# One shared score unit for the last two head groups of the last segment: 80 units in place of 81

## The chip, the cores and the metric

The kernel runs on one core of a Trainium2 chip. The metric is the device time of one execution in microseconds. A core has five engines that work side by side, each through its own instructions in order: TensorE (PE, matrix products), VectorE (DVE), ScalarE (ACT), GpSimd (POOL) and SyncE (SP, which here only issues DMA transfers). Their results meet in the on-chip memories SBUF and PSUM; an instruction that needs another engine's or a transfer's result waits on a semaphore.

## What is computed

One block of a model on 2048 tokens of width 640, in bf16. The tokens are normalised; `s` is an attention with 32 heads of width 20, in 4 segments of 512 tokens; `g` is a gated product of width 1536; the result is `x + s * g`.

```python
xn = layernorm(x)
for n in range(4):                       # segments of 512 tokens, 32 heads
    logits = q[n] @ k[n].T * scale + mask          # causal
    a_dot = softmax(logits) @ v[n]
    a_mem = (phi(q[n]) @ M) / (phi(q[n]) @ z + 1e-6)
    o[n] = g * a_mem + (1 - g) * a_dot             # g = sigmoid(beta), per head
    M, z = M + phi(k[n]).T @ v[n], z + sum(phi(k[n]))
s = o @ wo
h = sigmoid(xn @ w_gate) * (xn @ w_up)
out = x + s * silu(h @ w_down)
```

## The kernel before, in words

**Score units.** The 32 heads are 8 groups of 4. In a segment, a group has four key blocks of 128 keys; key block `kb` is seen by the queries from `128*kb` on, so the blocks have 512, 384, 256 and 128 query columns. Blocks are packed into units of up to 512 columns: block 0 alone, blocks 1 and 3 together, and block 2, which has 256 columns, together with block 2 of the neighbouring group. `pair_units` does this for two groups (5 units), `single_units` for one group (3 units, the last with 256 columns). For each unit, `scores` (L548) writes the products of four heads into the one PSUM tile `Sps`, `exps` has ScalarE take the exponential into a tile `pt` (L556, one instruction for the whole unit) and GpSimd mask each block's diagonal (L558).

**Using the units.** For all groups but the last two of the last segment, `attend_T` multiplies a group's `pt` tiles with the values once all its units are there, in the transposed form `ApsT` (L572); VectorE turns the result in blocks of 32 (L593), GpSimd and VectorE divide it, and VectorE turns it back into `obT` (L591). From there it goes to DRAM by `dot_spill` (L473) and back by `out_load` (L480, L483), as the left operand `oT` of the output product.

The last two groups of the last segment, 6 and 7, go another way, through `attend` (L612): unit by unit, into a PSUM tile `Aps` with queries on the partitions. When the group's fourth block is in, `finalize` (four VectorE instructions, L631 to L638) divides and adds the result to `odot`, which holds the memory part of the same rows. For group 7 `finalize` comes in two halves: the first two query blocks after the third key block, the others after the fourth.

**The tail.** `tail_spill` (L510) writes columns 384 to 511 of `odot` to DRAM, `tail_T` (L514) loads them transposed into `oTm`, `tail_sum` (L518, VectorE) adds what `oT` has for these rows. Columns 512 to 639 are transposed on TensorE by `tail_T4` (L523) and copied by ScalarE (L524). Then `tail_piece` makes the output product of the last segment in eight pieces of 128 tokens by 320 columns (L532, five matmuls each, the fourth with `oTm`), and multiplies it with `aa` on VectorE (L534). `tail_add` (L540) adds `x` and the rows are stored.

**The order of the work.** One slot belongs to each unit. A slot begins with the unit's scores and exponentials; the rest of it is filled with dense work from a queue: gate, up and down products of the four segments (5, 5 and 12 matmuls each; a down product is evacuated by a ScalarE instruction, L454, and then a VectorE one, L455). All else (projections, output products, spills, loads, the steps above) is an event with a time in slots; at its time in a slot, as a share of the slot's free work, it is put into the order. The planner has a cost for each piece of work; the sum over the number of slots is the `rate` that a slot is due.

```python
    SLOTS, SEG = len(units), 20
    LAST = (NSEG - 1) * SEG
    OLD = LAST + 15
    ...
    for slot in range(OLD, SLOTS - 1):
        at(slot + 1 + TIMES["attend"], 500, old_attend, slot)
    ...
    rate = (sum(k * c for _, k, c, _ in dense) + sum(e[2] for e in events) + AV_NS * len(visits)) / SLOTS
    ...
    fill(1e12)
    finish(held[1][3])
    tail_T4(0, 2)
    old_attend(SLOTS - 1)
    tail_piece(0, 0)
```

So the slots 75 to 80 hold the units of groups 6 and 7; `old_attend` of a unit comes 0.36 of a slot into the slot that follows its own, and the last unit's after all slots. The event times are written by hand in `TIMES`: of those in the last segment, `dot5` (`dot_spill` of groups 4 and 5) stands at slot 78.0, `load5` (their `out_load`) at 78.1, `add5` at 79.05. Segments 0 to 2 have 20 slots each before and after the change. The down products of the last 128 tokens are held back for the tail (`held`).

## Time and profile before

| what | value |
|---|---|
| median of 3 runs | 320.56 us (319.78 to 628.22) |
| profiled execution: span from the first to the last instruction | 317.6 us |
| what lies around the span, to the median | 2.96 us |
| TensorE busy | 309.7 us, 98% |
| VectorE, ScalarE, GpSimd busy | 229.5, 227.2, 135.5 us |
| granted TensorE clock | 0.999 |
| exponentials (L556) | 81, 150.3 us in all |
| slots 75 to 80 begin (first score matmul) | 285.23, 289.23, 291.81, 294.99, 298.08, 301.37 us |
| first matmul of the first output piece | 306.39 us |

The span is one execution taken by the hardware profiler; the runs are timed without it. An engine's busy time is no cost by itself: what counts is whether the engine that sets the end had to wait. In the lines of the trace, the first number is the start in us from the start of the span, the second the duration, and the bracket, where there is one, says how long the engine was idle before and what it waited for.

### The profile page before, as it was taken

The page shows a single profiled execution, that of the slowest core. Times are in us where ns is not written, and L with a number is a line of the kernel's source. Part 1 is how long each engine was busy: PE and PEld are TensorE (multiplying, and loading weights), DVE is VectorE, ACT ScalarE, POOL GpSimd, SP SyncE. Part 2 cuts the span into 40 slices and gives each one's busy share as a digit, 9 for nine tenths or more (in the row PEclk, how much of TensorE's full clock was granted, in tenths as well). Part 3 has the DMA queues.
Part 4 walks back from the last instruction along what each step waited for, and adds up shares of the span by engine and source line. Part 5 has one row for each costly group of instructions (what it writes and reads, how often), then busy time and mean ns, then how long its engine had stood idle before and what let it go on. Part 6 is the DMA issues. An engine that isn't in the chain of part 4 may idle for free.

```text
span 317.6 us, 10049 instructions
## 1 busy us (share of the span) xinstructions
PE 309.7 (98%) x4215; PEld 167.1 (53%) x4244; DVE 229.5 (72%) x505; ACT 227.2 (72%) x229; POOL 135.5 (43%) x230
## 2 busy tenths in 40 slices
PE   8999999999999999999999999999999999999995
PEld 3544445665555445654665455545466645445673
DVE  6474356755869888997779999977787686734565
ACT  3723477788898877778898868678897766777631
POOL 1870036535263445334453354444533353535322
PEclk9999999999999999999999999999999999999999
DMA  7984886420752462505954443238533000350302
GB/s 252 364 328 142 289 221 191 105 46 2 215 158 62 130 130 85 126 23 173 240 168 122 114 110 109 82 121 210 168 82 120 19 23 23 114 137 4 99 20 83
DMA packets 56085, 41.36 MB, mean 130 GB/s; under 512 B 26952, under 2 KB 54664, under 8 KB 56040
## 3 DMA queue, kind: packets, MB, share of 16 engines
q1 hardware_dynamic: 53496, 35.97, 39.7%
q10 hardware_dynamic: 2544, 4.75, 4.0%
q8 instruction: 33, 0.54, 0.7%
q14 instruction: 12, 0.10, 0.1%
HBM read 19.90 MB, written 14.78 MB: 109 GB/s over the span
## 4 chain that ended last, share of the span: by engine, by line
PE 96%; issue 1%; ACT 1%; DVE 1%; ACTq 0%
PE yp L130 11%; PE up L130 11%; PE gp L130 10%; PE psq L130 10%; PE Sps L548 9%; PE gp L134 6%; PE up L134 6%; PE yp L134 6%; PE psv L130 6%; PE ApsT L572 5%; PE psq L134 4%; PE sp L130 3%; PE sp L134 3%; PE sp L532 2%; PE psv L134 1%; PE wps L644 1%
## 5 line engine op out<-in xcount | busy, mean ns | idle before, releaser
L556 ACT ACTIVATE pt<-Sps 128x2048 bf16<-128x2048 f32 (+1 forms) x81 | 150.3, 1856 | 40.8 <-PE Sps L548 35.9
L558 POOL TENSOR_SCALAR_AFFINE_SELECT pt<-pt 128x512 bf16<-128x512 bf16 x128 | 83.2, 665 | 157.6 <-ACT pt L556 157.5
L438 DVE SCALAR_TENSOR_TENSOR hT<-tg,up 128x512 bf16<-128x512 bf16 x48 | 32.4, 675 | 23.2 <-PE up L130 8.7
L130 PE MATMUL up<-xnT,Wu 128*128 128x512 bf16 x147 | 40.3, 380 | 1.2 <-issue 1.0
L130 PE MATMUL yp<-Wd,hT 128*128 128x320 bf16 x257 | 40.1, 300 | 0.0
L427 ACT ACTIVATE tg<-gp 128x512 bf16<-128x512 f32 x48 | 28.6, 596 | 14.4 <-PE gp L130 11.0
L130 PE MATMUL gp<-xnT,Wg 128*128 128x512 bf16 x144 | 38.1, 379 | 0.3 <-issue 0.2
L548 PE MATMUL Sps<-QT,KT 23*128 23x128 bf16 (+3 forms) x512 | 32.6, 301 | 0.2
L591 DVE STREAM_TRANSPOSE obT<-ob 128x512 bf16<-128x512 bf16 x30 | 21.1, 705 | 13.4 <-POOL ob L587 13.3
L130 PEld LDWEIGHTS <-hT 128*128 128x128 bf16 x257 | 23.5, 98 | 11.6 <-issue 3.0
L455 DVE SCALAR_TENSOR_TENSOR aa<-t,yp 128x320 bf16<-128x320 bf16 x32 | 15.3, 480 | 13.8 <-ACT t L454 13.7
L134 PE MATMUL gp<-xnT,Wg 128*32 128x512 bf16 x360 | 24.1, 380 | 0.0
L548 PEld LDWEIGHTS <-KT 23*128 23x128 bf16 x512 | 10.0, 92 | 24.5 <-issue 24.1
L130 PEld LDWEIGHTS <-Wu 128*128 128x128 bf16 x160 | 14.3, 98 | 16.2 <-issue 3.2
L593 DVE STREAM_TRANSPOSE tb<-ApsT 128x512 f32<-128x512 f32 x30 | 21.2, 708 | 2.2 <-PE ApsT L572 2.1
L572 PE MATMUL ApsT<-pt,V 128*32 128x512 bf16 (+2 forms) x480 | 22.7, 299 | 0.0
L130 PEld LDWEIGHTS <-Wg 128*128 128x128 bf16 x150 | 14.1, 98 | 16.0 <-issue 1.9
L134 PE MATMUL up<-xnT,Wu 128*32 128x512 bf16 x320 | 21.7, 380 | 0.0
L454 ACT ACTIVATE t<-yp 128x320 bf16<-128x320 f32 x32 | 13.9, 435 | 10.2 <-PE yp L130 8.5
L130 PE MATMUL psv<-Wv,xnT 128*128 128x320 bf16 x130 | 20.6, 299 | 0.2
L587 POOL TENSOR_TENSOR ob<-tb,rb 128x320 bf16<-128x320 f32 x27 | 19.8, 733 | 2.3
L134 PE MATMUL yp<-Wd,hT 128*32 128x320 bf16 x508 | 20.0, 300 | 0.0
(122 smaller groups left out, 448.7 us busy)
## 6 DMA issues: line engine op xcount, KB each, us to landing
KT<-Kd SPq DMA_DIRECT2D x32, 80.0 KB
QT<-Qd SPq DMA_DIRECT2D x32, 80.0 KB
out_dram<-xt SPq DMA_DIRECT2D x14, 160.0 KB
Wg<-in_B_w_gate_dram ACTq DMA_DIRECT2D x1, 1920.0 KB
Wu<-in_B_w_up_dram ACTq DMA_DIRECT2D x1, 1920.0 KB
xt<-in_A_x_dram SPq DMA_DIRECT2D x3, 640.0 KB
Wd<-in_B_w_down_dram SPq DMA_DIRECT2D x1, 1920.0 KB
Xd<-xn SPq DMA_DIRECT2D x12, 160.0 KB
```

The lines of the kernel that those rows point to most:

```text
L130: nc.tensor.matmul(out_, lhsT=lhsT, rhs=rhs, start=start, stop=stop, skip_group_check=True)
L134: nc.tensor.matmul(out_[cols], lhsT=lhsT[:, cols], rhs=rhs, start=start, stop=stop, tile_position=(0, 32 * r), skip_group_check=True)
L427: nc.scalar.activation(tg[:], gp[:], ACT.Tanh, scale=0.5)
L438: nc.vector.scalar_tensor_tensor(out=h[:], in0=seg[n]["tg"][:], scalar=1.0, in1=up[:], op0=ALU.add, op1=ALU.mult)
L455: nc.vector.scalar_tensor_tensor(out=s["aa"][j][:, hs], in0=t2[:], scalar=1.0, in1=yp[:], op0=ALU.add, op1=ALU.mult)
L548: nc.tensor.matmul(Sps[:, r, c0:c0 + ncol], lhsT=KT[32 * r:32 * r + DH + 3, g, kb * P:(kb + 1) * P], rhs=QT[32 * r:32 * r + DH + 3, g, q0: ...
L556: nc.scalar.activation(pt[:, :, 0:ntot], Sps[:, :, 0:ntot], ACT.Exp, scale=SCALE)
L558: nc.gpsimd.affine_select(out=pt[:, :, c0:c0 + P], in_=pt[:, :, c0:c0 + P], compare_op=ALU.is_ge, fill=0.0, base=0, pattern=[[0, 4], [1, P ...
L572: nc.tensor.matmul(ps[32 * r:32 * r + 32, q0:L], lhsT=Vflat[n % 2][:, off:off + 32], rhs=t[:, r, c0:c0 + ncol], start=(i == 0), stop=(i == ...
L587: nc.gpsimd.tensor_tensor(ob[:, :, 0:DH], tb[:, :, 0:DH], rb[:].unsqueeze(2).to_broadcast([P, L // 32, DH]), op=ALU.mult)
L591: nc.vector.transpose(s["obT", g // 4][:, g % 4, :], ob[:].rearrange("p b e -> p (b e)"))
L593: s["turn", g] = (lambda: nc.vector.transpose(tb[:].rearrange("p b e -> p (b e)"), ps[:]), quotients, turn_back)
```

## The change

The last pair of groups in the last segment is packed like all the others: one unit holds the third key blocks (`kb` 2) of groups 6 and 7, where each had a unit of 256 columns. The list has 80 units. Group 7's blocks now come to `attend` in the order 2, 0, 1, 3 in place of 0, 1, 3, 2, and its last unit holds blocks 1 and 3. Two of the three tail events have other distances from the end.

```diff
-def single_units(g):
-    return [[(g, 0, 0, 512, 0)],
-            [(g, 1, 0, 384, 128), (g, 3, 384, 128, 384)],
-            [(g, 2, 0, 256, 256)]]
-
 def segment_units(n):
     units = []
     for g in range(0, NG, 2):
-        last = n == NSEG - 1 and g == NG - 2
-        units += single_units(g) + single_units(g + 1) if last else pair_units(g)
+        units += pair_units(g)
     return units
...
-    at(SLOTS - 2.001, 0, tail_spill)
-    at(SLOTS - 1.001, 0, tail_T)
+    at(SLOTS - 1.45, 0, tail_spill)
+    at(SLOTS - 0.9, 0, tail_T)
     at(SLOTS - 0.001, 0, tail_sum)
```

The lines after the slots stay as they are: `tail_T4(0, 2)` is in the order ahead of the last `old_attend`, which now holds both halves of group 7's `finalize`.

## The prediction

> **What bounds the kernel now.** I read first the page's busy times and the chain that ended last. They say the same: TensorE is busy nearly all the time, and the chain is made of its matmuls.

> ```profile
> PE 309.7 (98%) x4215; PEld 167.1 (53%) x4244; DVE 229.5 (72%) x505; ACT 227.2 (72%) x229; POOL 135.5 (43%) x230
> ...
> PE 96%; issue 1%; ACT 1%; DVE 1%; ACTq 0%
> ```

> So time is won only where a TensorE cost goes away, and lost wherever TensorE is made to wait. The list of waits shows how little it waits now: 1.2 us at the start, then nothing above 1.0 us in total. The granted clock is 0.999, so no clock effect stands behind this.

> Next I read the last 30 us in order of time, for each engine alone, because the change acts there. SyncE's queue first, then VectorE, ScalarE and TensorE (start, duration, instruction, idle time before it).

> ```profile
> 294.84 1.42 SPq L473 DMA_DIRECT2D OTd<-obT  x4
> ...
> 297.64 0.39 SPq L480 DMA_DIRECT2D oT<-OTd  x1
> 298.09 0.48 SPq L483 DMA_DIRECT2D oT<-OTd  x1
> 299.52 0.40 SPq L510 DMA_DIRECT2D Od<-odot  x1
> 301.69 1.16 SPq L514 DMA_TRANSPOSE oTm<-Od  x1
> ```

> ```profile
> 294.10 0.71 DVE L591 STREAM_TRANSPOSE obT<-ob 128x512 bf16<-128x512 bf16 x1 [1.25 <-POOL ob L587]
> ...
> 297.74 0.49 DVE L455 SCALAR_TENSOR_TENSOR aa<-t,yp 128x320 bf16<-128x320 bf16 x1 [2.50 <-ACT t L454]
> 298.14 0.25 DVE L631 RECIPROCAL rd<-Aps 128x16 f32<-128x16 f32 x1
> ...
> 299.17 0.33 DVE L638 TENSOR_TENSOR odot<-odot,od 128x320 bf16<-128x320 bf16 x1
> ...
> 306.12 0.42 DVE L518 TENSOR_TENSOR oTm<-oTm,oT 96x512 bf16<-96x512 bf16 x1 [0.51 <-DMA oTm<-Od]
> ```

> ```profile
> 295.50 1.88 ACT L556 ACTIVATE pt<-Sps 128x2048 bf16<-128x2048 f32 x1 [0.78 <-PE Sps L548]
> 297.27 0.43 ACT L454 ACTIVATE t<-yp 128x320 bf16<-128x320 f32 x1
> ```

> ```profile
> 296.28 0.35 PE L612 MATMUL Aps<-V,pt 128*128 128x21 bf16 x8
> ...
> 306.39 0.57 PE L532 MATMUL sp<-Wo,oT 128*128 128x320 bf16 x3
> ```

> The reader is to see one chain here. The attend that completes group 6 starts on TensorE at 296.28. `finalize` (L631 to L638) ends at 299.50, `tail_spill` (L510) is issued at 299.52, `tail_T` (L514) at 301.69, when the spill has landed, and `tail_sum` (L518) starts at 306.12, when the transposed block has landed. TensorE needs that block in the fourth matmul of the first output piece, at 306.80. This chain is 10.5 us long and ends 0.26 us before it is needed. It is invisible in the list of TensorE's waits, and it has no slack.

> **The change part by part.**

> *The merged unit.* The time from the last matmul before a unit to the first after it, less that last matmul's own streaming, is 0.318 us for either unit of 256 columns, 0.438 us for a unit of two 256-column blocks elsewhere in the trace, and 0.424 us for one of 512. Two units at 0.318 become one at 0.438: minus 0.20 us of TensorE. Nothing else leaves TensorE: the matmuls of `attend`, the gate, up and down products are all still there. On ScalarE two exponentials of 1.02 us become one of 1.88; ScalarE is 72% busy, so that is worth nothing by itself.

> *The planner's rate.* The planned work is 240.05 us over 81 slots, 2.964 us each; afterwards 239.55 over 80 (one `old_attend` of 0.5 less), 2.994 each. Dense work runs 31 ns per slot further ahead, 2.3 us by slot 75. I worked the planner's sums through for both lists; for the kernel before, the order that comes out is the trace's. Afterwards the order of segments 0 to 2 is the same but for a few matmuls that stand on the other side of an event. Cost: the next score unit waits for the exponential, which starts about 0.53 us after the scores and takes 1.88, so a slot under 2.46 us stalls. The shortest slots before are 2.46 to 2.62 us; afterwards slot 19 has 2.01 us planned, 2.45 with its scores. That is a stall of a tenth or two; I take 0.2 us in all, between 0 and 0.5.

> *The tail, one slot shorter.* Counted from the attend that completes group 6 (call it a; 296.28 before), TensorE's work up to the fourth matmul of the first piece was: 8 attend matmuls 0.20, 11 down matmuls 1.49 (0.136 each), scores 0.44, 7 down 0.95, 16 attend 0.41, 11 down 1.49, scores 0.32, 7 down 0.95, 16 attend 0.41, 23 down 3.12, two transposes 0.11, 8 attend 0.20, three pieces 0.41: 10.5 us, as the trace has it. Afterwards it is 0.20 + 1.49 + 0.44 + 0.95 + 24 attend 0.61 + 3.12 + 0.11 + 16 attend 0.41 + 0.41 = 7.7 us.

> *The chain in the new order.* `finalize` is no longer held: in the new order no down product is evacuated right ahead of it, so it starts at a + 0.36 and ends at a + 1.7 (1.36 long). But `tail_spill` is queued on SyncE behind `dot_spill(4,6)` and `out_load`, and these wait for group 5's last transpose (L591). In the new order that transpose stands behind the evacuation of a down product (L455), whose ScalarE half stands behind the merged unit's exponential, now 1.88 us. From slot 77's scores: exponential at 0.53, next ScalarE instruction 1.77 later (295.50 to 297.27 above), L455 0.47 after that, L591 0.41 later, 0.71 long: 3.9 us. SyncE is through with the loads 3.76 us after L591's end (294.81 to 298.57): 7.65. From slot 77's scores to a are 3.29 + 1.29 = 4.58 us. So `tail_spill` is issued at a + 3.1, nearly as late as before (a + 3.2), though a slot less is left.

> *Landing.* By the landing records the loads landed at 301.07, 2.98 us after the second was issued, and the spill 0.61 later. I take the same: loads at a + 5.6, spill and `tail_T` at a + 6.2. Were the spill not queued behind the loads it would land its own 2.16 us after issue, a + 5.3. The transpose's landing has two values in one row: 15 of its 16 engines landed 2.70 us after issue, the last at 4.33. That engine was carrying an instruction fetch of 16 KB at 303.96 to 305.00. [...] I take 2.70: a + 8.9. `tail_sum` with its start 0.52, and 0.2 to TensorE: a + 9.6. TensorE is there at a + 7.7 and **waits 1.9 us**, between 0 (spill not queued, L591 not late) and 3.5 (a fetch in the way of the transpose). No other work can fill it: the pieces are in order, and no dense work is left.

> [...]

> *Other edits.* The moved `tail_spill` and `tail_T` issue nothing earlier by themselves: SyncE's order is the same, nothing else is behind them before the output stores at 310, and both wait for data. `tail_T4(0,2)` is now issued ahead of the attend that holds group 7's first `finalize`; it waits for nothing, and the transposed copy of the first 256 tokens of the last segment lacks group 7's local part. The last attend has 16 matmuls and two halves of `finalize` on VectorE (1.03 us each, 307.15 to 308.18), one more than before behind `tail_sum`. VectorE idles 1.18 us before 310.16, which hides it; without that cover it costs up to 1.0. The last exponential is 1.88 us with two masks: ready about 4.4 us after its scores, needed after 5.1.

> **Sum.** Span 317.6 - 0.2 + 0.2 + 1.9 = 319.5. The median of the runs is 320.56, 2.96 above the span, so 322.5 us.

> **The rivals.**
> 1. *The chain keeps up.* If the spill isn't queued behind the loads (0.9 less) and L591 isn't late (1.1 less), the chain ends with TensorE and the change gives its 0.2: 320.4, not slower. For it: `finalize` itself comes 1.5 us earlier after a. Against: SyncE is in order, and the transposed block was only just in time with a slot more. 0.15.
> 2. *A fetch hits the spill or the transpose.* 1.1 to 1.6 more: 323.6 to 324.1. For it: the late sixteenth engine of the kernel before. [...] 0.22.
> 3. *Scores and exponentials in lockstep.* If the shifted dense work left the some 27 short slots behind an attend 0.2 us under 2.46, they would cost 5.4 us, with the tail 327.8: slower by over 2%. It decides at 2.0 us planned in a slot. Against: I find one such slot. 0.07.
> 4. *A unit's slot is saved,* some 3.3 us as slots are long now: 317.3. That the change makes nothing but 0.2 us go away speaks against it. 0.04, of which 0.01 for over 2% faster.

> The forecast itself has 0.52. The range 320.2 to 324.5 takes in rivals 1 and 2 and the bounds of the wait. Within 2% (6.4 us, about what a measurement of this kernel tells from no change) lie all but rival 3 and a little of rival 4: faster 0.01, same 0.92, slower 0.07.

> **What would show it.** In the changed profile: a TensorE wait before the fourth matmul of the first piece, put down to `tail_sum` (L518) or its DMA; L591 of group 5 behind an L455; L510 issued right after L483 rather than after L638; L514 about 2.2 to 3.1 us behind it; slots before 75 as long in sum as before. The prediction is wrong if L518 ends before TensorE comes to the first piece, or if TensorE's waits grow in segments 0 to 2.

## The result and the profile after

The changed kernel takes 328.24 us (median of 5 runs, 327.77 to 329.14) against 320.08 before: a ratio of 1.0261, with a 95% interval of 1.0239 to 1.0282. It is 8.2 us slower; 1.9 were forecast (322.5 against 320.56). One of the five runs before took 628.22 us; the ratio leaves it out. The profiled execution has a span of 327.4 us, 9.8 more than the one before. It is the slowest of its five runs, and lies 1.7 us below its own time, as the spans of the other four do.

The changed kernel computes a little less: as the prediction says, its transposed copy of the first 256 tokens of the last segment lacks group 7's local part. This holds for experiments 4 to 8, 10 and 11 too; experiments 9 and 12 compute all of it.

The page of the changed kernel, engines and the chain that ended last:

```profile
PE 315.4 (96%) x4289; PEld 168.0 (51%) x4289; DVE 230.6 (70%) x505; ACT 226.8 (69%) x228; POOL 135.2 (41%) x230
...
PE 79%; DVE 8%; ACT 5%; issue 3%; DMA 3%; POOL 2%; SPq 0%; ACTq 0%; DVEq 0%
```

Before, the chain was 96% TensorE; now a sixth of it runs over VectorE, ScalarE and transfers. The list of TensorE's waits (engine, line, what it waited for: us in total, times, longest) names them:

```profile
PE Aps L606 <- DVE od L630: 2.8, 1, 2.8
PE wps L638 <- DVE mn L149: 1.2, 1, 1.2
PE yp L128 <- issue: 1.1, 1, 1.1
PE am L124 <- DVE hT L432: 0.8, 1, 0.8
PE po L517 <- DVE aa L449: 0.7, 1, 0.7
PE Sps L542 <- ACT pt L550: 0.6, 1, 0.6
PE yp L124 <- DVE aa L449: 0.3, 1, 0.3
PE sp L128 <- ACT tg L421: 0.2, 1, 0.2
```

(Line numbers are six lower than before.) Only L638's wait, at the very start, was there before; the list before begins:

```profile
PE wps L644 <- DVE mn L155: 1.2, 1, 1.2
PE up L130 <- issue: 1.0, 6, 0.2
```

The reader is to see that the new waits are of two kinds: two in the tail (L606, L517), and five small ones spread over the segments, where the list before had nothing above 0.2 us at a time.

**Where the 9.8 us lie.** Slot by slot, I took the start of the scores in both traces and subtracted what the planner itself shifted. What remains is 0.34 us at slot 0 (the start of the execution), then steps at slots 14 (0.7), 21 to 23 (0.3), 36 (0.4), 43 (1.1), 59 (1.4), 63 to 66 (0.9) and small ones that cancel: 5.0 by slot 75. (A wait inside a slot shows as a later start of the next one: the steps at slots 43 and 59 are waits in slots 42 and 58.) From there to the end it is 5.0 more, less the 0.2 of the merged unit.

**The tail.** Queue and engines in order of time, of the changed kernel: SyncE, VectorE, TensorE.

```profile
305.89 0.39 SPq L474 DMA_DIRECT2D oT<-OTd  x1
306.34 0.48 SPq L477 DMA_DIRECT2D oT<-OTd  x1
306.86 1.54 SPq L504 DMA_DIRECT2D Od<-odot  x1
310.61 1.16 SPq L508 DMA_TRANSPOSE oTm<-Od  x1
```

```profile
301.95 0.49 DVE L449 SCALAR_TENSOR_TENSOR aa<-t,yp 128x320 bf16<-128x320 bf16 x1 [2.20 <-ACT t L448]
302.35 0.70 DVE L585 STREAM_TRANSPOSE obT<-ob 128x512 bf16<-128x512 bf16 x1
...
310.14 0.96 DVE L481 TENSOR_TENSOR oT<-oT,oTm 128x1536 bf16<-128x1536 bf16 x1 [3.94 <-DMA oT<-OTd]
...
313.28 0.42 DVE L512 TENSOR_TENSOR oTm<-oTm,oT 96x512 bf16<-96x512 bf16 x1 [1.39 <-DMA oTm<-Od]
313.67 0.49 DVE L449 SCALAR_TENSOR_TENSOR aa<-t,yp 128x320 bf16<-128x320 bf16 x1
...
314.51 0.32 DVE L630 TENSOR_TENSOR od<-Aps,rd 128x160 bf16<-128x160 f32 x1
```

```profile
311.55 0.27 PE L517 MATMUL po<-ident,odot 128*128 128x128 bf16 x2 [0.74 <-DVE aa L449]
311.66 0.45 PE L606 MATMUL Aps<-V,pt 128*128 128x21 bf16 x12
314.89 0.26 PE L606 MATMUL Aps<-V,pt 128*128 128x21 bf16 x4 [2.78 <-DVE od L630]
315.00 0.96 PE L526 MATMUL sp<-Wo,oT 128*128 128x320 bf16 x3
315.75 0.47 PE L526 MATMUL sp<-Wo,oTm 128*128 128x320 bf16 x1
```

The attend that completes group 6 is at a = 303.83. The spill is issued right behind the loads at a + 3.0, `tail_T` at a + 6.8, `tail_sum` (L512) ends at a + 9.9: this is the chain that was forecast, 0.5 us later. The lateness goes with an instruction fetch of 16 KB, which the transfer list has from 306.74 to 308.18: of the sixteen landing records that each of these transfers leaves, the spill's last came 0.6 us after the fifteenth, and the loads' 0.8 to 0.9. In experiment 8, where no fetch met them, `tail_T` was issued at a + 6.1. But TensorE does not wait at the fourth matmul of the first piece. It waits ahead of the pieces, at the last four matmuls of the last attend, for L630: the first half of group 7's `finalize`, which reads the same PSUM tile and stands behind `tail_sum` on VectorE. So the fourth matmul comes at a + 11.9 in place of 7.7. And the pieces then run at half speed: three matmuls take 0.96 us in place of 0.57. By the records of the granted clock it fell to 0.5 at 314.25 and stayed there for 3.41 us.

From that fourth matmul to the last matmul were 6.83 us before and 7.67 now. The tail's 5.0 us are thus 2.3 of late transfers (7.7 to 10.1, `tail_sum`'s end and 0.2), 1.9 of the held attend (10.1 to 11.9) and 0.8 at half clock.

### The profile page after: what moved, and what is told of

Its sections match the earlier page's. It is cut to its first block, busy times and chain, and to the rows that moved or that the text cites. A ratio compares the mean times of both kernels' runs of the same rounds, so it can differ in the third digit from the quotient of the medians.

```text
span 327.4 us, 10164 instructions
## 1 busy us (share of the span) xinstructions
PE 315.4 (96%) x4289; PEld 168.0 (51%) x4289; DVE 230.6 (70%) x505; ACT 226.8 (69%) x228; POOL 135.2 (41%) x230
## 4 chain that ended last, share of the span: by engine, by line
PE 79%; DVE 8%; ACT 5%; issue 3%; DMA 3%; POOL 2%; SPq 0%; ACTq 0%; DVEq 0%
PE gp L124 9%; PE up L124 9%; PE yp L124 8%; PE psq L124 8%; PE Sps L542 7%; PE yp L128 6%; PE psv L124 5%; PE up L128 5%; PE gp L128 5%; PE ApsT L566 4%; ACT pt L550 4%; PE psq L128 3%; PE sp L124 2%; PE sp L526 2%; PE sp L128 2%
## 5 line engine op out<-in xcount | busy, mean ns | idle before, releaser
L550 ACT ACTIVATE pt<-Sps 128x2048 bf16<-128x2048 f32 x80 | 150.1, 1877 | 47.5 <-PE Sps L542 45.9
L432 DVE SCALAR_TENSOR_TENSOR hT<-tg,up 128x512 bf16<-128x512 bf16 x48 | 32.4, 675 | 23.5 <-PE up L124 8.8
L124 PE MATMUL gp<-xnT,Wg 128*128 128x512 bf16 x158 | 41.9, 380 | 0.0
L124 PE MATMUL up<-xnT,Wu 128*128 128x512 bf16 x149 | 38.9, 380 | 0.0
L124 PE MATMUL yp<-Wd,hT 128*128 128x320 bf16 x245 | 38.3, 300 | 0.3 <-DVE aa L449 0.3
L542 PE MATMUL Sps<-QT,KT 23*128 23x384 bf16 (+3 forms) x512 | 32.5, 300 | 0.8 <-ACT pt L550 0.6
L585 DVE STREAM_TRANSPOSE obT<-ob 128x512 bf16<-128x512 bf16 x30 | 21.1, 705 | 12.4 <-POOL ob L581 12.1
L124 PEld LDWEIGHTS <-hT 128*128 128x128 bf16 x245 | 22.5, 98 | 11.3 <-issue 3.2
L449 DVE SCALAR_TENSOR_TENSOR aa<-t,yp 128x320 bf16<-128x320 bf16 x32 | 15.2, 478 | 16.2 <-ACT t L448 15.8
L128 PE MATMUL up<-xnT,Wu 128*32 128x512 bf16 x364 | 24.8, 380 | 0.0
L448 ACT ACTIVATE t<-yp 128x320 bf16<-128x320 f32 x32 | 13.7, 435 | 14.2 <-PE yp L124 10.2
L128 PE MATMUL yp<-Wd,hT 128*32 128x320 bf16 x556 | 22.1, 300 | 1.1 <-issue 1.1
L128 PE MATMUL gp<-xnT,Wg 128*32 128x512 bf16 x328 | 22.9, 380 | 0.0
L542 PEld LDWEIGHTS <-KT 23*128 23x128 bf16 x512 | 10.1, 92 | 24.8 <-issue 24.3
L566 PE MATMUL ApsT<-pt,V 128*32 128x512 bf16 (+3 forms) x480 | 22.7, 299 | 0.0
L587 DVE STREAM_TRANSPOSE tb<-ApsT 128x512 f32<-128x512 f32 x30 | 21.2, 708 | 1.6 <-PE ApsT L566 1.3
```

Source lines behind the costliest of these rows:

```text
L124: nc.tensor.matmul(out_, lhsT=lhsT, rhs=rhs, start=start, stop=stop, skip_group_check=True)
L128: nc.tensor.matmul(out_[cols], lhsT=lhsT[:, cols], rhs=rhs, start=start, stop=stop, tile_position=(0, 32 * r), skip_group_check=True)
L432: nc.vector.scalar_tensor_tensor(out=h[:], in0=seg[n]["tg"][:], scalar=1.0, in1=up[:], op0=ALU.add, op1=ALU.mult)
L449: nc.vector.scalar_tensor_tensor(out=s["aa"][j][:, hs], in0=t2[:], scalar=1.0, in1=yp[:], op0=ALU.add, op1=ALU.mult)
L542: nc.tensor.matmul(Sps[:, r, c0:c0 + ncol], lhsT=KT[32 * r:32 * r + DH + 3, g, kb * P:(kb + 1) * P], rhs=QT[32 * r:32 * r + DH + 3, g, q0: ...
L550: nc.scalar.activation(pt[:, :, 0:ntot], Sps[:, :, 0:ntot], ACT.Exp, scale=SCALE)
```

## The experiments

Times are compared with runs of the kernel before that share the chip; their medians were 319.4 to 320.0 us.

**1. The order of the segments alone** (`e1_order_1039`). The kernel before with the changed kernel's rate in slots 0 to 59:

```diff
-        due += rate
+        due += rate * (1.01039 if slot < 60 else 0.95844 if slot < 75 else 1.0)
```

> The kernel before with its 81 units and its own tail; only the planner's rate is 1.039% higher in slots 0 to 59, as in the changed kernel, and 4.2% lower in slots 60 to 74, which gives the work back before the tail. Theory 'order' (the shifted dense work alone makes TensorE wait some 5 us in segments 0 to 2): slot 60 begins 4.0 us later than the planned shift, as in the changed kernel, and the time is 324.1 to 324.7 us. Rival 'tail' (all of the loss lies after slot 74, what was seen before it belongs to that one execution): 320.1.

Measured: 322.09 us, ratio 1.0082 (1.0069 to 1.0095): 2.7 us slower, between what the two theories gave, with no change at all in the units or the tail. The waits stand where those of the changed kernel stand:

```profile
PE Sps L548 <- ACT pt L556: 0.8, 2, 0.6
PE am L130 <- DVE hT L438: 0.8, 1, 0.8
```

TensorE's idle time at slot 14 is 0.63 us in both kernels, and that at slot 42 is 0.81 here and 0.82 in the changed kernel. The 1.4 us at slot 58 are missing. In experiments 5, 6 and 7, which have the same order there, at most 0.2 us is lost: the wait belonged to the one profiled execution of the changed kernel. Its cause stays open. (The instruction fetch just ahead of it began 440 TensorE instructions after the one before; in no other case of these traces were there more than 396. One case doesn't show that a fetch was late.) The waits at slots 62, 63 and 65, which this kernel doesn't have, came back in experiments 5 to 8, at 0.43, 0.14 and 0.39 us from one matmul to the next, less the streaming of the first. So the order costs some 2.3 us net up to slot 59 and 0.9 after it, 3.2 in all. This is an estimate, added up from gaps of several profiles; the times of the changed kernel and experiment 4, compared through their ratios, give 2.1, and 3.3 if one adds what experiment 4 has for itself, a wait of 0.7 in the segments and a tail that is 0.5 longer in its profile.

**2. and 3. Other shifts** (`e2_order_1005`, `e3_order_0995`), the same edit with 1.005 and 0.995:

> The kernel before with the planner's rate 0.5% higher in slots 0 to 59, and 2% lower in slots 60 to 74. Theory 'a cost that grows with the shift': about half of what 1.039% costs, 322 to 322.5 us. Theory 'single collisions' (each wait comes from two particular pieces of work that now stand too close): any value between 320.1 and 324.7, with the waits at places other than at 1.039%.

> The kernel before with the planner's rate 0.5% lower in slots 0 to 59, and 2% higher in slots 60 to 74: dense work later in place of earlier. If running ahead is what costs (less dense work left to cover the projections' slots): 320.1. If it is single collisions, which either direction can bring: 320.5 to 324.

Measured: 324.88 (ratio 1.0155, 1.0138 to 1.0172) and 326.07 (1.0189, 1.0173 to 1.0206). Half the shift costs nearly twice as much, 4.9 us, and a shift to the other side more still, 6.1 (both above the ranges that were expected for single collisions, by 0.2 and 2.1 us). TensorE's longest waits at 1.005 and then at 0.995:

```profile
PE sp L130 <- DVE aa L455: 1.6, 1, 1.6
...
PE up L130 <- DVE hT L438: 0.6, 1, 0.6
```

```profile
PE sp L134 <- DVE oT L487: 1.1, 1, 1.1
...
PE psv L130 <- DVE aa L455: 0.8, 1, 0.8
PE yp L134 <- DVE hT L438: 0.7, 1, 0.7
```

The longest waits are others, at other places; the one at slot 14 is there at 1.005 too, 0.6 us long. A cost that grows with the shift falls; single collisions are what is left and fit the lists: a matmul's PSUM tile is given out while VectorE or ScalarE is still busy with something that now stands ahead of its evacuation.

**4. The tail alone** (`e4_tail_only`). The changed kernel with the order of before up to slot 74:

```diff
-        due += rate
+        due += 2963.5967 if slot < 75 else rate + 75 * (rate - 2963.5967) if slot == 75 else rate
```

> The changed kernel with its 80 units, but slots 0 to 74 are planned at the rate of the kernel before, and slot 75 takes up the difference of 2.3 us; the order from slot 76 on is that of the changed kernel. As in the changed kernel, the transposed copy of the first 256 tokens of the last segment lacks group 7's local part. Theory 'order': no waits before slot 74, the tail's 3.2 to 5 us stay: 323.2 to 325. Rival 'the tail costs what was predicted' (1.7 us): 321.8. Rival 'all is tail': 328.2.

Measured: 325.50, ratio 1.0195 (1.0178 to 1.0211), 6.1 us, half a microsecond above what the theory 'order' gave. The segments' waits are gone, but for one of 0.7 us between matmuls at slot 39, without a named cause, that the kernel before doesn't show. From a to the last matmul it takes 20.1 us (19.6 in the changed kernel, 17.4 before), with the same two waits, 2.7 and 1.3 us, and the same clock drop of 3.41 us. The tail accounts for 5 to 6 us; "the tail costs what was predicted" falls.

**5. One finalize** (`e5_one_finalize`). No attend matmul stands behind a `finalize`:

```diff
-            split = g == NG - 1
+            split = False
```

> The changed kernel with group 7 finalized in one piece after its fourth block, so that no attend matmul stands behind a finalize (the same local part is left out as in the changed kernel). Theory 'held attend' (TensorE's longest wait, 2.8 us, is for the first half of finalize, which stands behind tail_sum on VectorE): TensorE then waits at the fourth matmul of the first piece, until 0.2 us after tail_sum, 1.5 to 2 us earlier: 326.2 to 326.7. Rival 'the transfer alone': the wait moves to the piece and its end stays: 328.2.

Measured: 325.88, ratio 1.0194 (1.0179 to 1.0208), some 2.1 us less than the changed kernel's ratio gives. The wait is now where it was predicted, at the fourth matmul, and that comes at a + 9.75 in place of 11.93. Not all of this is won: the clock falls here too, at 312.17, and from that matmul to the last it takes 8.41 us, where it took 7.67 in the changed kernel and 6.73 in experiment 7 at full clock. Its trace, TensorE:

```profile
309.98 0.57 PE L526 MATMUL sp<-Wo,oT 128*128 128x320 bf16 x3
311.77 0.31 PE L526 MATMUL sp<-Wo,oTm 128*128 128x320 bf16 x1 [1.23 <-DVE oTm L512]
```

**6. The spill from another queue** (`e6_spill_act`).

```diff
-        nc.sync.dma_start(Od[(NSEG - 1) % 2][:, C3:C4].rearrange("(j p) d -> p j d", p=P),
+        nc.scalar.dma_start(Od[(NSEG - 1) % 2][:, C3:C4].rearrange("(j p) d -> p j d", p=P),
```

> The changed kernel with tail_spill issued from ScalarE's queue in place of SyncE's (the same local part is left out as in the changed kernel). Theory 'queue' (the spill is late because it is queued on SyncE behind the loads of groups 4 and 5): it is issued 1.7 us after the attend that completes group 6 in place of 3.0, lands by 4.0, tail_sum ends near 7.3 us, before TensorE needs it at 7.7: the tail's waits go, 323.5 to 324. Rival 'the DMA engines are busy with the loads anyway': the spill lands 0.5 us earlier at most: 327.7.

Measured: 327.72, ratio 1.0252 (1.0221 to 1.0283); its six runs scatter from 325.50 to 329.63, so the time doesn't decide. The profile, of the fastest run, shows the spill issued at a + 2.0 (1.7 expected), but `tail_T` only at a + 5.7 and not 4.0; the queues of ScalarE and of SyncE:

```profile
304.62 0.45 ACTq L504 DMA_DIRECT2D Od<-odot  x1
```

```profile
308.32 1.16 SPq L508 DMA_TRANSPOSE oTm<-Od  x1
```

The packets of the spill ran from 305.60 to 307.88, between those of the loads (305.84 to 308.57). `tail_sum` comes 1.1 us earlier than in the changed kernel and TensorE's wait is 1.7 in place of 2.8. Of these 1.1 us some 0.6 go with the fetch that met the spill there: against experiment 8, where none did, `tail_T` comes only 0.4 us earlier. So the theory 'queue' falls, and the rival's half a microsecond is about right; the packets of the spill and the loads ran side by side, which fits its reason. Of the six runs the fastest alone has a mean clock of 1.0, the others 0.995; why those scatter over 3 us stays open.

**7. TensorE kept busy in the wait** (`e7_warm`).

```diff
                 finalize(n, g, 0, 2)
+                for _ in range(12):
+                    nc.tensor.matmul(Sps[:, 0, :], lhsT=ident[:], rhs=Wu[:, 0, 0:L], start=True, stop=True)
```

> The changed kernel with 12 more TensorE products of 512 columns between the two parts of the last attend, written where nobody reads them; they take 2.6 of the 2.8 us in which TensorE waits (the same local part is left out as in the changed kernel). Theory 'clock' (the granted clock is halved because TensorE stood still, and the first pieces run at 0.26 us per matmul in place of 0.136): the pieces run at 0.136, 1.2 us earlier: 327.0. Rival 'something else slows the pieces' (operands, PSUM): 328.2 or a little above.

Measured: 327.72, ratio 1.0251 (1.0219 to 1.0283), runs from 326.83 to 330.36, again too scattered for a difference of a microsecond. In the profile the clock does not fall, and the same pieces run at full speed:

```profile
314.17 0.25 PE L606 MATMUL Aps<-V,pt 128*128 128x21 bf16 x4 [0.20 <-DVE od L632]
314.27 0.57 PE L526 MATMUL sp<-Wo,oT 128*128 128x320 bf16 x3
314.68 0.30 PE L526 MATMUL sp<-Wo,oTm 128*128 128x320 bf16 x1
```

From the fourth matmul to the last it takes 6.73 us, where the changed kernel took 7.67: 0.9 us by the clock. "Something else slows the pieces" falls.

**8. Three collisions moved** (`e8_three_places`).

```diff
-                    at(t0 + t, 0, fn, *a)
+                    at(t0 + t + (0.5 if n == 0 and (name, i) == ("phi_k", 1) and fn is phi_exp else 0.0), 0, fn, *a)
...
-            on("mem", MEM_NS, mem_part, *[(n, i % 4, i // 4) for i in range(8)])
+            for i in range(8):
+                at(t0 + TIMES["mem"][i] + (0.3 if (n, i) == (2, 5) else 0.0), MEM_NS, mem_part, n, i % 4, i // 4)
...
-        ORDER["columns"] = slot + 1 in visits
+        ORDER["columns"] = slot + 1 in visits and slot != 58
```

> The changed kernel with three pieces of work moved in the segments: the second exponential of phi of the keys half a slot later in segment 0; one memory product (half 1, rows 128 to 255, segment 2) 0.3 slot later; and the dense work of slot 58 in whole matmuls in place of four column parts, 120 instructions less (the same local part is left out as in the changed kernel). Theory 'single collisions': the waits of 0.7, 1.1 and 1.4 us at slots 14, 43 and 59 go, each by its own move: 325.0. Rival for the third: the wait there isn't for instructions, and stays: 326.4. Rival for all: the waits come up elsewhere: 328.

Measured: 327.00, ratio 1.0209 (1.0189 to 1.0229). The wait at slot 14 is gone by its one move. That at slot 42 only changed its name: the idle time of 0.82 us ahead of `am` became 0.17 there and 0.58 ahead of the next `gp`. Slot 58 has no wait, but neither had it in experiments 1 and 5, so nothing follows for its cause. The time lies between what the theory (325.0) and the last rival (328) gave. And this execution's tail is a microsecond longer: TensorE waits 4.5 us at the held attend, because fifteen of `tail_T`'s landing records were in by a + 8.8 and the sixteenth at a + 10.3; the transfer list has an instruction fetch of 16 KB there, from 310.07 to 311.13. That fits the second rival of the prediction, a fetch that hits the transpose, in another kernel.

**9. to 12. Put right.** Four versions with 80 units and the order of before in the segments. Two edits recur. The first is the rate of the kernel before in all 80 slots, which leaves 2.46 us of down products for the time after the last slot; the second is the one `finalize` of experiment 5.

```diff
-        due += rate
+        due += 2963.5967
```

With the rate alone (`e11_old_rate_only`):

> The changed kernel with one edit: the planner's rate of the kernel before in all 80 slots; group 7 is finalized in two halves, as in the changed kernel (and the same local part is left out). Theory: the transfers are no longer late, so the last four attend matmuls wait only for the first half's own VectorE work, some 0.75 us from the attend on: 0.7 to 1 us above the run with one finalize, 320.1 to 320.5 with the kernel before at 319.4. Rival (the held attend costs only while tail_sum is late): no difference, 319.5.

Measured: 321.09, ratio 1.0052 (1.0033 to 1.0071). `tail_sum` is done at a + 8.4, before TensorE comes, and still the attend is held, for its own `finalize`:

```profile
305.83 0.45 PE L606 MATMUL Aps<-V,pt 128*128 128x21 bf16 x12
307.61 0.25 PE L606 MATMUL Aps<-V,pt 128*128 128x21 bf16 x4 [1.32 <-DVE od L630]
```

With the one `finalize` too (`e10_old_rate`):

> The changed kernel with the planner's rate of the kernel before in all 80 slots, so that 2.46 us of down products are left for the time after the last slot, and group 7 finalized in one piece (the same local part is left out as in the changed kernel). Theory: the segments' waits go, and the tail has 2.5 us more between the attend that completes group 6 and the pieces, 10.2 us, against 9.9 for the transfers: no clock drop, 320 to 321. Rival (tail_sum, which stands ahead of the left down products' evacuations on VectorE, holds PSUM): 1 to 2 us of wait, 321.5 to 323.

Measured: 319.47, ratio 0.9996 (0.9981 to 1.0010): the whole loss is gone. TensorE's list of waits begins with L638's 1.2 us at the start and has nothing else above 0.6, and all of that lies in the first 16 us:

```profile
PE wps L638 <- DVE mn L149: 1.2, 1, 1.2
PE psv L124 <- DVE xnT L664: 0.6, 1, 0.6
```

With all of the computation (`e12_complete`: the same two edits, the tail's order as below, `tail_sum` out of the slots), and with the edits of experiments 4 and 6 in place of the old rate (`e9_repaired`):

```diff
     finish(held[1][3])
+    old_attend(SLOTS - 1)
+    for _ in range(FC - 1):
+        next(held[0][3])
     tail_T4(0, 2)
-    old_attend(SLOTS - 1)
+    tail_T4(2, 4)
+    tail_sum()
+    finish(held[0][3])
     tail_piece(0, 0)
     tail_piece(0, 1)
     tail_add(0, 0, 2, nc.gpsimd, nc.sync)
-    finish(held[0][3])
     tail_piece(1, 0)
     tail_piece(1, 1)
     tail_add(1, 0, 1, nc.vector)
-    tail_T4(2, 4)
     tail_piece(2, 0)
```

> The changed kernel's 80 units with all of the computation in it: the planner's rate of the kernel before in all slots, group 7 finalized in one piece, its transposes behind that and behind 11 matmuls of the last held down product, tail_sum behind them too. Theory: no TensorE wait over 0.3 us after slot 75; the merged unit's 0.2 us and no more: 319.2 to 319.8 with the kernel before at 319.4. Rival (the finalize of 1.36 us isn't covered, or the held product is missed later): 320.3 or more.

> The changed kernel's 80 units, all of the computation in it, with four edits: slots 0 to 74 at the rate of the kernel before; tail_spill from ScalarE's queue; group 7 finalized in one piece and its transpose behind it, covered by the last held down product, which now comes ahead of the pieces; tail_sum behind that finalize. Theory (the segments' order, the late transfers and the held attend are all of the loss): no TensorE wait over 0.3 us after slot 75, and the 0.2 us of the merged unit are left: 319.5 to 320.2 with the kernel before at 320.0. Rival (the merged unit itself makes the tail too short): 322 or more.

Measured: 320.33, ratio 1.0014 (1.0002 to 1.0026), and 321.63, ratio 1.0064 (1.0050 to 1.0079). The first has one wait left in the tail, 0.4 us, for the one `finalize`. The second waits 1.2 us in the tail, ahead of the last held down product, for an evacuation that stands behind the sum of the loaded blocks on VectorE, and 0.7 for the one `finalize`. So neither kept to the 0.3 us that was expected, and the second missed its range by over a microsecond. Both executions also waited 0.6 and 1.0 us at slot 39. So 80 units can be had at about the price of 81, with all of the computation for 0.1% more, and no version here is faster than the kernel before.

## Why the prediction was wrong, point by point

The forecast was right that the kernel gets slower, and in the chain of transfers. One of its own signs of being wrong came true: TensorE's waits grew in the segments. The terms, in their order:

- **The merged unit, minus 0.2 us:** nothing contradicts it, and nothing here can show it. With nearly all waits out of the way the units give no measurable gain (0.9996), and 0.2 us would be 0.06%.
- **The planner's rate, 0.2 us, between 0 and 0.5:** the step that failed first. It cost some 3.2 us, by the estimate under experiment 1; the part that experiment 1 measured by itself is 2.7. The order itself was worked out rightly, "the same but for a few matmuls that stand on the other side of an event"; the price was not. I priced only the score units' wait for the exponential, by slot length; slot 19, where I expected it, was 2.54 us long and has none. At slot 14 it was that wait, though not in a short slot: the score exponential before it (L550, at 82.98) stood behind another exponential (L365, 1.27 us), which had waited 0.74 us for VectorE. The other waits for which the profile names a cause (at slots 42, 62 and 65) are for an instruction that empties a PSUM tile. All of TensorE's results but the scores take turns in the four PSUM buffers of this kernel's pool `ps_d`, so a matmul can wait for an evacuation that has nothing to do with its own data; for this I had no term. The lines of the changed kernel that show one, VectorE and TensorE at slot 42, with the evacuation (L432) right behind a transpose:

```profile
179.61 0.66 DVE L585 STREAM_TRANSPOSE obT<-ob 128x512 bf16<-128x512 bf16 x1
180.19 0.65 DVE L432 SCALAR_TENSOR_TENSOR hT<-tg,up 128x512 bf16<-128x512 bf16 x1
```

```profile
180.89 0.33 PE L124 MATMUL am<-Mbd,qtd 128*128 128x84 bf16 x3 [0.82 <-DVE hT L432]
```

- **The tail one slot shorter, and the chain:** right in mechanism and place: L585 behind L449, the spill right behind the loads, `tail_sum` late. The term was 1.9 us; the transfers measured 2.3. The 0.4 more go with the fetch, which came at a + 2.9, where it met the loads and the spill; `tail_T`, for which I took 2.70 us, landed after 2.58. No run shows that the place of a fetch can be counted ahead: in the trace of before they began 153 to 377 TensorE instructions apart, weight loads among them. Nor does a run show that the spill lands behind the loads because it is queued behind them: a + 6.2 took the 0.61 us from the trace of before, and the spill issued from ScalarE's queue (experiment 6) brought `tail_T` only 0.4 us ahead of experiment 8.
- **"It waits for nothing" and "VectorE idles 1.18 us, which hides it":** the step that failed second. `tail_T4` itself waited 0.74 us for L449. Above all, I followed what the second half of `finalize` delays on VectorE, and not that the last attend's own last four matmuls wait for the first half. In the kernel before, 23 down matmuls stood between the first half and the attend behind it, and covered it. This cost 1.9 us behind the late `tail_sum`, and 1.3 by itself (experiment 11).
- **The clock:** no term at all. "No clock effect stands behind this" was right of before, and a wait of 1.9 us was forecast without asking what it does to the clock: 0.8 us in the profiled execution (7.67 in place of 6.83), and 0.9 by experiment 7.
- **From span to time:** 2.96 us were taken; the runs after show 1.7. In the 11 executions of the kernel before that ran beside experiment 1, time and span also lie 1.7 apart, so the first median, of only 3 runs, was about a microsecond high for that span.
- **The rivals:** over 2% slower had 0.07, with lockstep of scores and exponentials as its mechanism. That was not it: the changed kernel has one such wait, of 0.6 us. A fetch beside the transpose did not come in the profiled execution of the changed kernel (its loads and its spill met one instead, for 0.4 to 0.6 us) and did in experiment 8, where the last landing record is 1.5 us behind the fifteenth.

3.2 + 2.3 + 1.9 + 0.8 - 0.2 = 8.0 us, of 8.2 measured between the medians. The terms come from single profiled executions, and the first is an estimate, so that the sum comes out this close is partly luck.

## What to carry to other kernels

In a kernel whose bounding engine never waits, a hand-made order is itself a result: a change to a planner's rate re-orders everything before the place that was edited, and must be priced by the slack of each buffer's release or, better, kept out by holding the rate. When two parts of one accumulation lose the work that stood between them, look at the second part's wait for the first part's reader. And when a wait on TensorE is forecast, ask next what it does to the clock.

## What the runs showed of the hardware

The clock records of the changed kernel come in steps of 3.41 us: the drop lasts one, the full clock ahead of it 307.20 us, which is 90, and that behind it 10.24, which is 3. In the trace of before the full clock lasts 310.61 us, 91 of them. The clock of a step goes, in these traces, with TensorE's work in the step before. Busy time and clock in two such cases, first with one finalize (clock falls), then with the spill on ScalarE's queue (it doesn't); columns: stretch, its length, busy us of PE, PEld, DVE, ACT, POOL, granted clock, DMA share, GB/s.

```profile
305.30:308.80 3.50, 3.50 (x46) 2.66 (x43) 0.74 (x1) 1.69 (x3) 1.23 (x2) 1.00 0.57 170
308.80:312.20 3.40, 1.71 (x26) 1.02 (x25) 1.92 (x6) 0.70 (x2) 0.00 (x0) 1.00 0.17 39
312.20:315.60 3.40, 3.40 (x15) 1.91 (x13) 1.94 (x6) 0.00 (x0) 1.27 (x1) 0.50 0.01 2
```

```profile
307.50:310.90 3.40, 2.66 (x30) 1.86 (x28) 1.75 (x3) 1.25 (x4) 1.17 (x2) 1.00 0.35 99
310.90:314.30 3.40, 1.76 (x17) 1.30 (x17) 3.10 (x12) 0.09 (x1) 0.00 (x0) 1.00 0.01 2
314.30:317.70 3.40, 3.40 (x27) 2.33 (x25) 1.78 (x5) 0.81 (x2) 1.39 (x1) 1.00 0.13 48
```

TensorE is idle for about 1.7 us of the middle stretch in both, in two pieces of 0.46 and 1.23 us in the first and in one of 1.61 in the second. So the longest idle time doesn't decide: the kernel with the longer one kept its clock. Nor does the busy share. It is 0.51 of the step in the first and 0.53 in the second (by the steps' exact ends), but experiment 9 kept the full clock after a step that was busy for 0.41 (from 315.29 us), and experiment 5 itself after one of 0.44 (from 319.00).

The second surprise is how often a transfer ends late where an instruction fetch of 16 KB runs beside it. In the changed kernel `tail_T` waited for the last of the spill's sixteen landing records: it was issued at 310.61, 0.02 us after the spill's sixteenth record and 0.6 after its fifteenth. With a fetch running, the fifteenth and the sixteenth record of `tail_T` are 1.5 us apart in experiment 8, and 1.6 in the kernel before, where TensorE happened not to be waiting. Over all fourteen traces, of the 413 transfers after the first 10 us that such a fetch overlapped, 147 had a last record over 0.5 us behind the fifteenth; of the 664 others, 25. The traces don't name the DMA engine, so that the fetch and the late record share one, as the prediction has it, is inferred.
